# Soft-MoE after attention on one core: last combine weights turned ahead of the stores, two evictions by one engine each, first quarters from two queues, 16 constant products less

## The chip, the cores and the metric

The kernel runs on one core of a Trainium2 chip. The metric is the device time of one execution in microseconds; the median of three runs is given. One further execution was profiled, and all views below are of that one.

## The reference

```python
def attn(q, k, v, cap):                      # (8 batches, 12 heads, 448 rows, 64 columns)
    scores = cap * tanh(q @ k.T / sqrt(64) / cap)
    return softmax(scores) @ v

def soft_moe(x, phi, w1, w2):                # x: 3584 x 768, 8 experts, 4 slots each, F = 1024
    logits = x @ phi                         # 3584 x 32
    d = softmax(logits, axis=0)              # dispatch weights, over the tokens
    slot_in = d.T @ x                        # 32 x 768
    slot_out[e] = relu(slot_in[e] @ w1[e]) @ w2[e]
    c = softmax(logits, axis=1)              # combine weights, over the slots
    return c @ slot_out                      # 3584 x 768, float32
```

The tokens `x` are the attention's output with its heads side by side. The output has 11.0 MB.

## The kernel before

The order of instructions is written out by hand (`tc.manual_schedule()`); the framework adds the semaphore waits. Each engine runs its own list in order: PE (TensorE), DVE (VectorE), ACT (ScalarE), POOL (GpSimd) and SP, which computes nothing and issues DMAs. A DMA issued by SP or ACT signals its landing on one of eight semaphores (DMAHW0 to DMAHW7), which the framework gives out in turn.

**Attention**, to about 245 us. Two heads of a batch make a pair; scores come in 112 chunks of 3 x 448 columns. ACT takes tanh (L325) and exp (L329) of each chunk, DVE takes part of the exp by a polynomial, and PE multiplies scores and values and turns the results. `FILL` lists constant products (`fill`, 57 columns each, L425) that PE does between others: for seven of the batches 38 in one place and 12 in another.

**Per batch b**, `phi` gives logits, ACT their exp `E`, and `e_rep` (POOL, L488) repeats it into the tile `e4`, of which there is one buffer. `e_transp(b)` (L502) turns `e4` by four PE transposes into PSUM (`eps`, L507) and copies it by DVE (L508) into `ET4`, or for the last two batches (`bl - 1` and `bl`, 6 and 7) into `ETl`: these are the combine weights, not yet normalised. `e_sums` (L513) adds them up by seven small products (`wps`, L517) and takes the reciprocal into `winv`. For the last two batches all this is done late: batch 7 first, then `e_rep` builds `e4` of batch 6 anew.

**The slot network**, from about 246 us. `busy(6)` does two constant products of 384 columns while PE waits. `layer1` gives four results `hp` (two groups of four experts by two halves of F); `relu` evicts each into `hbs` (in the tile `small`); the one with `i == half == 1` is split, 288 columns by ACT and 224 by DVE. `h_transp` turns them (`hps`, `hpad`). `layer2(n0, half)` adds up `so_ps[half]`, the slots' output for columns 0 to 383 or 384 to 767, in 16 steps of four products. Their weights are partly kept in SBUF (`w2b`) and partly loaded back from DRAM by 21 DMAs of 384 KB on SP (`w2t`, L824): ten of half 0, then eleven of half 1, the last of them being `n0 = 60` of half 1, which the last step of `layer2` needs.

**The stores.** There are 28 tiles of 128 tokens. For tiles 0 to 11 each half is stored by itself (`half_tile`: one product `op`, one eviction times `winv` by ACT or DVE into `obh`, one DMA of 192 KB on SP from L898). Half 0 of tiles 0 to 9 is done between the steps of `layer2(..., 1)`:

```python
    act.copy(so[0][:, 0:HB], so_ps[0][:, 0:HB])
    dve.tensor_copy(so[0][:, HB:HD], so_ps[0][:, HB:HD])
    ...
        layer2(n0, 1)
        if n0 % 8 == 4 and n0 != n2 // 2 + 4 and done < NHL:
            for eng in ("act", "dve") if n0 < n2 // 2 else ("act",):
                half_tile(done, 0, ...)
```

Half 0 of tile 0 is cut once more into two quarters of 96 KB, one evicted by ACT and one by DVE (L915), both stored by SP (L916). Then come `so[1]` (DVE, L944), half 0 of tiles 10 and 11, and in the last loop half 1 of tiles 0 to 11. Tiles 12 to 27 are done whole: two products, one eviction of 768 columns (ACT L980, DVE L978) into `ob`, and nine DMAs of one or two tiles on SP. In this loop, between tiles, stand `e_transp(7)`, `e_rep(6)`, `e_transp(6)` and `e_sums(3)`.

Of the kernel before, what the change touches and what calls it, by code (L numbers as in the profile page):

```python
# [10 lines left out]
BF16 = mybir.dt.bfloat16  # L11
# [3 lines left out]
ALU = mybir.AluOpType  # L15
ACT = mybir.ActivationFunctionType
PSUM = bass.MemoryType.PSUM

P = 128
HP = 64  # L20
NT = 7
# [16 lines left out]
def kernel(  # L38
# [12 lines left out]
    B, H, _, _ = q.shape  # L51
    D = H * DH
# [4 lines left out]
    HD = D // 2  # L57
# [12 lines left out]
    pe, dve, act, pool, sp = nc.tensor, nc.vector, nc.scalar, nc.gpsimd, nc.sync  # L70

    consts = ctx.enter_context(tc.tile_pool(name="consts", bufs=1))
    wts = ctx.enter_context(tc.tile_pool(name="wts", bufs=1))
    psT = ctx.enter_context(tc.tile_pool(name="psT", bufs=1, space=PSUM))
# [14 lines left out]
    phib = consts.tile([P, NJ, NS], BF16, name="phib")  # L89
    ET4 = consts.tile([P, B // 2 - 1, NT, 2, HP], BF16, name="ET4")  # L90
    winv = consts.tile([P, B // 2, NT], F32, name="winv")
    slT = consts.tile([P, NJ, NS], BF16, name="slT")
    zacc = consts.tile([P, 1], F32, name="zacc")
    rz = consts.tile([P, 1], F32, name="rz")
# [390 lines left out]
    def e_rep(b):  # L485

        e4s[b] = consts.tile([P, NG, 4 * NS], BF16, name="e4", tag="e4", bufs=1)
        pool.tensor_copy(e4s[b].rearrange("p g (a s) -> p g a s", a=4),  # L488
                         es[b].unsqueeze(2).to_broadcast([P, NG, 4, NS]))
# [9 lines left out]
        else:  # L499
            dve.tensor_tensor(zacc, ps, zacc, op=ALU.add)  # L500

    def e_transp(b):  # L502

        ps = psT.tile([P, 512], BF16, name="eps", tag="T")
        for g in range(NG):
            n = P if g < NF else HP
            pe.transpose(ps[:, g * P:g * P + n], e4s[b][0:n, g, :], ident[0:n, 0:n])  # L507
        dve.tensor_copy((ETl if b >= B - 2 else ET4[:, b // 2])[:, :, b % 2, :],  # L508
                        ps[:, 0:S].rearrange("p (c q) -> p c q", q=HP))

    def et_tile(bb, c):
        return (ETl if bb == B // 2 - 1 else ET4[:, bb])[:, c, :, :].rearrange("p a q -> p (a q)")

    def e_sums(bb):
        ps = psT.tile([P, NT], F32, name="wps", tag="T")
        for c in range(NT):
            pe.matmul(ps[:, c:c + 1], et_tile(bb, c), ones32, start=True, stop=True)  # L517
        dve.reciprocal(winv[:, bb, :], ps)
# [34 lines left out]
    def at(j, slot, f, *a):  # L553
        if j < 0:
            j, slot = 0, "b"
        aux.setdefault((j, slot), []).append((f, a))
# [2 lines left out]

        busy(n, psV.tile([P, parts * P], F32, name="junk", tag="pv"))  # L560

    FILL = ((4, 'a', fill, 6), (5, 'a', fill, 6), (6, 'a', spare, 3), (6, 'c', spare, 9), (7, 'a', fill, 38), (8, 'a', fill, 12), (9, 'a', fill, 4),)
    PER = 2 * NQB * NT // CH
    assert PER == 7 and NQB == 3

# [12 lines left out]
    for b in range(B):  # L578
        j, p = b * PER, 6 * b
# [10 lines left out]
        if b == 0:  # L590
            at(j + 1, "d", spare, 34)
            at(j + 2, "d", spare, 4)
        for k, slot, f, n in FILL:
            if (b or k > 2) and j + k < NCH - 1:
# [39 lines left out]
    def busy(n, home=None, by=None):  # L634
        home, by = junk if home is None else home, ones if by is None else by
        if home.shape[-1] > P:
            for _ in range(n // 3):
                pe.matmul(home, ones, wide, start=True, stop=True)
            n, home = n % 3, home[:, 0:P]
        for _ in range(n):  # L640
            pe.matmul(home, by, by, start=True, stop=True)
# [51 lines left out]
    Q, bl = NQ - 1, B - 1  # L693
# [2 lines left out]
    attp.close()  # L696
    mid = ExitStack()
    big = mid.enter_context(tc.tile_pool(name="big", bufs=1, space=PSUM, reuse_waits="tile"))
    turns = [0, 1, 2, 6, 3, 4, 5, 0, 6, 3, 0, 1, 2, 3, 4, 5]

    def bank(shape, dt=F32, name="bank"):
        n = turns.pop(0)
        if not turns:
            turns.extend((3, 2, 6, 0, 1))
        return big.tile(shape, dt, name=name, tag=f"b{n}")
# [84 lines left out]
    phi_last(last - 1, (0, 1, 2))  # L790
    x_last(1, dve.tensor_copy)
    phi_last(last, (0, 1), True)
    busy(6)
    e_last(0)
    phi_last(last, (2,))
    phi_last(last - 1, (NF,))
# [22 lines left out]
    tl = ctx.enter_context(tc.tile_pool(name="tl", bufs=1, reuse_waits="tile"))  # L819
# [6 lines left out]

    hpad = tl.tile([P, E, NFT, NS], BF16, name="hpad")
    pool.memset(hpad, 0.0)
    ETl = tl.tile([P, NT, 2, HP], BF16, name="ETl")

    def w2_half(n, half):
        part = (n - n % 4, half)
        if part in w2t:
# [3 lines left out]
    hbs = {}  # L837
# [8 lines left out]
        return i, half, hp  # L846

    def relu(i, half, hp):
        f0, f1, mid = 512 * half, 512 * half + 512, 512
        if i == half == 1:  # L850
            mid = f0 + 288
        if f0 < mid:
            f2 = min(f1, mid)
            act.activation(hbs[i][:, f0:f2], hp[:, 0:f2 - f0], ACT.Relu, scale=rz)
        if mid < f1:
            f2 = max(f0, mid)
            dve.tensor_scalar(hbs[i][:, f2:f1], hp[:, f2 - f0:512], rz, 0.0, ALU.mult, ALU.max)

    def h_transp(i):

# [10 lines left out]
    so_ps = []  # L871

    def layer2(n0, half):
        for n in range(n0, n0 + 4):
            i, ft, gg = blocks[n]
            pe.matmul(so_ps[half][32 * gg:32 * gg + NS, :],  # L876
                      hpad[:, 4 * i + gg, ft, :],
                      w2_half(n, half),
                      start=(n0 == 0), stop=(n0 == len(blocks) - 4))
# [7 lines left out]
    so = [small[:, 2 * F + n * HD:2 * F + n * HD + HD] for n in range(2)]  # L887
    for hp in first:
        relu(*hp)
# [13 lines left out]
    def half_tile(n, half, home, eng):  # L903

        m = half * NH + n
        if m % 8 == 0:
            obs[m // 8] = own_home([P, 8, HD], F32, "obh")
        ob = obs[m // 8][:, m % 8, :]
        bb, c = divmod(n, NT)
        if n == half == 0:  # L910

            for p, (bank_p, mul) in enumerate(zip(home, (act.mul, dve.tensor_scalar_mul))):
                cs = slice(p * HD // 2, (p + 1) * HD // 2)
                pe.matmul(bank_p, et_tile(bb, c), so[half][:, cs], start=True, stop=True)
                mul(ob[:, cs], bank_p, winv[:, bb, c:c + 1])  # L915
                sp.dma_start(out=bass.AP(tensor=out.tensor, offset=cs.start,  # L916
                                         ap=[[NT * D, P], [1, HD // 2]]), in_=ob[:, cs])
            return
        pe.matmul(home, et_tile(bb, c), so[half], start=True, stop=True)
        if eng == "dve":  # L920
            dve.tensor_scalar_mul(ob, home, winv[:, bb, c:c + 1])
        else:
            act.mul(ob, home, winv[:, bb, c:c + 1])
        store(n, half, half + 1, ob)

    NH, NHL = 12, 10
    n2 = len(blocks)
    for n0 in range(0, n2, 4):
        if n0 == n2 // 2 - 8:
            h_transp(1)  # L930
        layer2(n0, 0)
    HB = HD // 2
    act.copy(so[0][:, 0:HB], so_ps[0][:, 0:HB])
    dve.tensor_copy(so[0][:, HB:HD], so_ps[0][:, HB:HD])
    done = 0
    for n0 in range(0, n2, 4):
        layer2(n0, 1)

        if n0 % 8 == 4 and n0 != n2 // 2 + 4 and done < NHL:
            for eng in ("act", "dve") if n0 < n2 // 2 else ("act",):  # L940
                half_tile(done, 0, bank([P, HD], name="op0") if done else
                          [bank([P, HD // 2], name="op00") for _ in range(2)], eng)
                done += 1
    dve.tensor_copy(so[1], so_ps[1])  # L944
    for done in range(NHL, NH):
        half_tile(done, 0, bank([P, HD], name="op0"), "dve" if done % 2 else "act")
    mid.close()
# [3 lines left out]
    last_ob = None  # L951
    for n in range(B // 2 * NT):
        bb, c = divmod(n, NT)
        if n == NH + 3:
            e_transp(B - 1)
            e_rep(B - 2)
        if n == NH + 5:
            e_transp(B - 2)
        if n == NH + 7:
            e_sums(B // 2 - 1)  # L960
        op = fin.tile([P, 2, 512], F32, name="op", tag="op")
        if n < NH:
            half_tile(n, 1, op[:, 0, 0:HD], "act" if n % 2 else "dve")
            continue
        for half in range(2):
            pe.matmul(op[:, half, 0:HD], et_tile(bb, c), so[half],
                      start=True, stop=True)

        if n == NH or c == 0 or full:
            n1 = n  # L970
            if n in (NH, NH + 4, NH + 8, NH + 11):
                ob, at0 = own_home([P, 4, 2, HD], F32, "ob"), n
                last_ob = ob if n == NH + 8 else last_ob
        if n == B // 2 * NT - 1:
            ob, at0 = last_ob, n - 3
        dst = ob[:, n - at0, :, :]
        if n % 2:
            dve.tensor_scalar_mul(dst, op[:, :, 0:HD], winv[:, bb, c:c + 1])  # L978
        else:
            act.mul(dst, op[:, :, 0:HD], winv[:, bb, c:c + 1])  # L980
        full = n > n1 or c == NT - 1
        if full:
            store(n1, 0, 2, ob[:, n1 - at0:n - at0 + 1, :, :].rearrange("p t a d -> p (t a d)"),
                  n - n1 + 1)
# [35 lines left out]
```

## Time and profile before

| | us |
|---|---|
| median of 3 runs (295.8 to 296.04) | 296.0 |
| the profiled execution, its own time | 295.63 |
| its span, first to last instruction | 293.9 |
| PE busy | 255.3 (87%) |
| DVE busy | 240.0 (82%) |
| ACT busy | 260.1 (89%) |
| POOL busy | 138.6 (47%) |
| mean DMA rate | 232 GB/s |

All times in the views are counted from the span's start. The difference of 1.7 us between span and own time lies around the span. The page cuts the span into 40 slices and gives the busy share of each in tenths. A window's row gives, after its length, the busy time of PE, PEld (weight loads), DVE, ACT and POOL with the number of instructions, the granted PE clock, the DMA share and GB/s. In a source view the three durations are the least, the median and the largest in ns. A name with a q (SPq) is the engine's sequencer, here issuing DMAs.

### The profile page before, as it was taken

The numbers are of one execution on the slowest core, as the hardware profiler recorded it, in microseconds if no ns is written. First come the engines' busy times: TensorE is split into PE (matmuls) and PEld (weight loads), VectorE is DVE, ScalarE is ACT, GpSimd is POOL, SyncE is SP. The second block draws the span as 40 slices with busy tenths as digits, with TensorE's granted clock in tenths as the row PEclk, the third lists the DMA queues.
The fourth block names the chain that finished last, engine by engine and source line by source line (L and its number), as shares of the span: only waits on it lengthen the run. The fifth ranks groups of instructions, "written<-read, shape, count | busy, mean of one in ns | idle before, by whom it ended". The sixth has DMA issues, their size and how long they took to land.

```text
span 293.9 us, 10841 instructions
## 1 busy us (share of the span) xinstructions
PE 255.3 (87%) x4728; PEld 173.8 (59%) x4728; DVE 240.0 (82%) x554; ACT 260.1 (89%) x211; POOL 138.6 (47%) x200
## 2 busy tenths in 40 slices
PE   8898889988998899879988998899989899998800
PEld 6656566756675667556756675667566668542400
DVE  3728998999999999999999989998999976246920
ACT  4999999999999999999999999999999997237710
POOL 4493555763677366735673658375643220300000
PEclk9999999999999999999999999999999999999975
DMA  7999999999999999999999999999999576979996
GB/s 230 249 196 205 221 180 216 199 189 218 229 219 203 204 229 222 203 200 223 193 191 217 209 221 202 217 219 225 209 183 216 108 245 217 406 307 393 356 420 283
DMA packets 58560, 68.13 MB, mean 232 GB/s; under 512 B 4240, under 2 KB 54672, under 8 KB 58512
## 3 DMA queue, kind: packets, MB, share of 16 engines
q0 software_dynamic: 42448, 35.31, 78.1%
q1 hardware_dynamic: 15776, 31.89, 31.1%
q8 instruction: 37, 0.61, 0.8%
q10 hardware_dynamic: 288, 0.23, 0.2%
q14 instruction: 11, 0.09, 0.1%
HBM read 91.72 MB, written 19.27 MB: 378 GB/s over the span
## 4 chain that ended last, share of the span: by engine, by line
DVE 36%; PE 35%; ACT 17%; issue 4%; POOL 2%; DMA 1%; DVEq 0%
PE pv L395 12%; ACT ex L325 8%; ACT ex L329 7%; PE sc L316 6%; DVE xq L405 4%; DVE ex L376 3%; DVE xp L375 3%; DVE xp L372 3%; DVE xp L373 3%; DVE kT L278 3%; DVE ex L369 3%; DVE xp L374 3%; DVE xf L371 2%; DVE qT L278 2%; PE so_ps L876 2%
## 5 line engine op out<-in xcount | busy, mean ns | idle before, releaser
L325 ACT ACTIVATE ex<-sc 128x1344 f16<-128x1344 f32 (+1 forms) x113 | 147.6, 1414 | 1.7 <-PE sc L316 1.6
L329 ACT ACTIVATE ex<-ex 128x1792 bf16<-128x1792 f16 (+5 forms) x58 | 119.7, 2068 | 0.1
L395 PE MATMUL pv<-vbd,ex 128*128 128x130 bf16 (+1 forms) x1610 | 94.5, 211 | 5.7 <-POOL vbd L286 3.2
L395 PEld LDWEIGHTS <-ex 128*128 128x128 bf16 (+1 forms) x1680 | 75.7, 101 | 33.5 <-PE sc L316 7.0
L316 PE MATMUL sc<-qT,kT 64*64 64x448 bf16 x672 | 70.3, 359 | 4.0 <-DVE qT L278 1.6
L286 POOL CAST vbd<-vraw 64x896 bf16<-64x896 f32 x46 | 44.0, 956 | 52.5 <-PE pv L395 37.9
L316 PEld LDWEIGHTS <-kT 64*64 64x64 bf16 x672 | 24.4, 105 | 10.2 <-issue 5.8
L405 DVE TENSOR_TENSOR xq<-pv,rec 128x448 bf16<-128x448 f32 x46 | 28.7, 625 | 1.6
L117 POOL DMA_DIRECT2D w1b<-in_moe_w_dram x32 | 25.3, 792 | 0.0
L488 POOL COPY e<-E 128x512 bf16<-128x512 bf16 x9 | 6.4, 708 | 37.1 <-PE eps L507 19.7
L376 DVE TENSOR_TENSOR ex<-ex,xp 128x896 uint16<-128x896 uint16 (+1 forms) x39 | 21.8, 559 | 1.2
L294 POOL MEMSET vbd<- 64x1 bf16 x22 | 3.1, 139 | 41.1 <-PE pv L395 41.1
L375 DVE TENSOR_TENSOR xp<-xp,xf 128x896 f16<-128x896 f16 (+1 forms) x39 | 22.0, 563 | 0.4
L373 DVE TENSOR_TENSOR xp<-xp,xf 128x896 f16<-128x896 f16 (+1 forms) x39 | 21.6, 554 | 0.7
L276 PE MATMUL qps<-ident,qb 128*64 128x128 bf16 x308 | 12.8, 221 | 8.8 <-DVE kT L278 6.4
L278 DVE COPY kT<-kps 128x896 bf16<-128x896 bf16 x23 | 14.3, 622 | 6.2 <-PE kps L276 5.8
L372 DVE TENSOR_SCALAR xp<-xf 128x896 f16<-128x896 uint16 (+1 forms) x39 | 18.9, 484 | 0.5
L276 PEld LDWEIGHTS <-qb 128*64 128x64 bf16 x308 | 10.9, 109 | 14.0 <-issue 13.5
L425 PE MATMUL pv<-ones 128*128 128x57 bf16 x474 | 18.6, 188 | 0.0
L186 POOL DMA_DIRECT2D qb<-in_q_dram x22 | 16.7, 761 | 3.2 <-DMA kraw<-in_k_dram 3.2
L457 DVE COPY xT<-xps 128x896 bf16<-128x896 bf16 (+1 forms) x24 | 14.4, 598 | 3.3 <-PE xps L448 3.1
L121 POOL DMA_DIRECT2D w2d<-in_moe_w_dram x21 | 16.4, 811 | 0.0
(135 smaller groups left out, 365.1 us busy)
## 6 DMA issues: line engine op xcount, KB each, us to landing
w1b<-in_moe_w_dram POOLq DMA_DIRECT2D x32, 384.0 KB, 8.4
vraw<-in_v_dram SPq DMA_DIRECT2D x44, 224.0 KB, 6.0
w2d<-in_moe_w_dram POOLq DMA_DIRECT2D x21, 384.0 KB, 8.9
w2t<-w2d SPq DMA_DIRECT2D x21, 384.0 KB, 7.2
out_dram<-ob SPq DMA_DIRECT2D x7, 768.0 KB, 7.8
qb<-in_q_dram POOLq DMA_DIRECT2D x22, 224.0 KB, 7.3
kb<-in_k_dram POOLq DMA_DIRECT2D x22, 224.0 KB, 6.1
out_dram<-obh SPq DMA_DIRECT2D x23, 192.0 KB, 2.1
```

Of the source, the lines that this page charges most:

```text
L117: pool.dma_start(out=w1b[e][:, js, fs], in_=w1r[:, e, js, fs])
L278: dve.tensor_copy(t, ps)
L286: pool.tensor_copy(vbds[Q % 2][r, :, :, c0:c0 + DH], raw[r])
L316: pe.matmul(sc[cs, u, 0:S], qkT["k", Q][r, c, cs], qkT["q", Q][r, :, cs], start=True, stop=True)
L325: act.activation(exs[j][:, half * CS + u0:half * CS + u1, :].bitcast(F16), sc[:, u0:u1, 0:S], ACT.Tanh, scale=qk_scale / cap)
L329: act.activation(exs[j][:, u0:u1, :], exs[j][:, u0:u1, :].bitcast(F16), ACT.Exp, scale=cap)
L372: lambda: dve.tensor_scalar(p, f, c3, c2, ALU.mult, ALU.add),
L373: lambda: dve.tensor_tensor(p, p, f, op=ALU.mult),
L375: lambda: dve.tensor_tensor(p, p, f, op=ALU.mult),
L376: lambda: dve.tensor_tensor(y, y, p, op=ALU.add),
L395: pe.matmul(out_, exs[j][r, u, q0:q0 + (HP if tail else P)], v_, start=(c == 0 and g == gs[0] < NF), stop=(c == NT - 1), skip_group_check= ...
L405: dve.tensor_tensor(xq[Q][:, h, s0:s1, :], pv[:, 0:s1 - s0, 0:DH], rec.to_broadcast([P, s1 - s0, DH]), op=ALU.mult)
```

## The change

- The two last combine weights are turned earlier: `e_transp(6)` takes the place of `busy(6)`, before `e4` is overwritten; `e_transp(7)` stands between the copy of `so[0]` and the first store, and `e_sums(3)` behind the copy of `so[1]`, ahead of tiles 10 and 11. The second `e_rep(6)` goes. `ETl` moves to another pool.
- The relu of `i == half == 1` and the copy of `so[0]` are each ACT's alone.
- The first quarter's store is issued by ACT, the second's by SP.
- Half 0 of tiles 0 to 9 stands ahead of two steps of `layer2(..., 1)` instead of behind them.
- `FILL` has 37 and 11 products for 38 and 12, in seven batches each. With the two of `busy(6)` that makes 16 products less in the program (or 20, counted in units of 128 columns for those two).

```diff
+    ETl = consts.tile([P, NT, 2, HP], BF16, name="ETl")
...
-    def e_transp(b):
-        ps = psT.tile([P, 512], BF16, name="eps", tag="T")
+    def e_transp(b, ps=None):
+        if ps is None:
+            ps = psT.tile([P, 512], BF16, name="eps", tag="T")
...
-    FILL = (... (7, 'a', fill, 38), (8, 'a', fill, 12), (9, 'a', fill, 4),)
+    FILL = (... (7, 'a', fill, 37), (8, 'a', fill, 11), (9, 'a', fill, 4),)
...
-    turns = [0, 1, 2, 6, 3, 4, 5, 0, 6, 3, 0, 1, 2, 3, 4, 5]
+    turns = [0, 1, 2, 6, 3, 4, 5, 0, 6, 3, 2, 0, 1, 2, 3, 4, 5]
...
-    busy(6)
+    e_transp(bl - 1, bank([P, 512], BF16, name="eps"))
...
-    ETl = tl.tile([P, NT, 2, HP], BF16, name="ETl")
...
     def relu(i, half, hp):
-        f0, f1, mid = 512 * half, 512 * half + 512, 512
-        if i == half == 1:
-            mid = f0 + 288
-        ...
+        dst = hbs[i][:, 512 * half:512 * half + 512]
+        if i or not half:
+            act.activation(dst, hp, ACT.Relu, scale=rz)
+        else:
+            dve.tensor_scalar(dst, hp, rz, 0.0, ALU.mult, ALU.max)
...
-                sp.dma_start(out=bass.AP(tensor=out.tensor, offset=cs.start,
+                (act, sp)[p].dma_start(out=bass.AP(tensor=out.tensor, offset=cs.start,
...
-    HB = HD // 2
-    act.copy(so[0][:, 0:HB], so_ps[0][:, 0:HB])
-    dve.tensor_copy(so[0][:, HB:HD], so_ps[0][:, HB:HD])
+    act.copy(so[0], so_ps[0])
+    e_transp(bl)
     for n0 in range(0, n2, 4):
-        layer2(n0, 1)
-        if n0 % 8 == 4 and n0 != n2 // 2 + 4 and done < NHL:
+        if n0 % 8 == 0 and n0 != n2 // 2 and done < NHL:
             for eng in ("act", "dve") if n0 < n2 // 2 else ("act",):
                 half_tile(done, 0, ...)
+        layer2(n0, 1)
     dve.tensor_copy(so[1], so_ps[1])
+    e_sums(bl // 2)
...
-        if n == NH + 3:
-            e_transp(B - 1)
-            e_rep(B - 2)
-        if n == NH + 5:
-            e_transp(B - 2)
-        if n == NH + 7:
-            e_sums(B // 2 - 1)
```

More of the change, by code (lines that the diff above doesn't have):

```diff
@@ L560, in spare @@
         busy(n, psV.tile([P, parts * P], F32, name="junk", tag="pv"))
-    FILL = ((4, 'a', fill, 6), (5, 'a', fill, 6), (6, 'a', spare, 3), (6, 'c', spare, 9), (7, 'a', fill, 38), (8, 'a', fill, 12), (9, 'a', fill, 4),)
+    FILL = ((4, 'a', fill, 6), (5, 'a', fill, 6), (6, 'a', spare, 3), (6, 'c', spare, 9), (7, 'a', fill, 37), (8, 'a', fill, 11), (9, 'a', fill, 4),)
     PER = 2 * NQB * NT // CH
@@ L848, in relu @@
     def relu(i, half, hp):
-        f0, f1, mid = 512 * half, 512 * half + 512, 512
-        if i == half == 1:
-            mid = f0 + 288
[L852 to L857, printed above, removed]
+        dst = hbs[i][:, 512 * half:512 * half + 512]
[3 more added lines that the diff above has]
+            dve.tensor_scalar(dst, hp, rz, 0.0, ALU.mult, ALU.max)
     def h_transp(i):
@@ L915, in half_tile @@
                 mul(ob[:, cs], bank_p, winv[:, bb, c:c + 1])
-                sp.dma_start(out=bass.AP(tensor=out.tensor, offset=cs.start,
-                                         ap=[[NT * D, P], [1, HD // 2]]), in_=ob[:, cs])
+                (act, sp)[p].dma_start(out=bass.AP(tensor=out.tensor, offset=cs.start,
+                                                   ap=[[NT * D, P], [1, HD // 2]]), in_=ob[:, cs])
             return
```

## The prediction

> **What bounds the kernel now.** I read the page first (slices, queues), then windows of one microsecond over the last stage, then the timeline and the source views of the stores.
>
> ```profile
> ACT  4999999999999999999999999999999997237710
> DMA  7999999999999999999999999999999576979996
> q8 instruction: 37, 0.61, 0.8%
> ```
>
> The last line gives packets, MB and share of queue 8. Up to about 245 us ScalarE is full (its exp and tanh groups, L325 and L329, show 1.7 and 0.1 us of idle time), so nothing done to TensorE there can gain much. The last stage is the one that changes, and it ends 13 us after the last arithmetic (DVE L978 ends at 280.9): it is the draining of stores that sets the end.
>
> ```profile
> 260.00:261.00 1.00, 0.90 (x21) 0.40 (x10) 0.24 (x1) 0.32 (x1) 0.00 (x0) 1.00 1.02 412
> 262.00:263.00 1.00, 1.00 (x16) 0.29 (x12) 0.91 (x2) 0.58 (x1) 0.00 (x0) 1.00 0.38 123
> 263.00:264.00 1.00, 1.00 (x12) 0.23 (x10) 0.72 (x2) 0.58 (x1) 0.00 (x0) 1.00 0.31 103
> 267.00:268.00 1.00, 0.83 (x3) 0.23 (x4) 1.00 (x3) 0.68 (x2) 0.00 (x0) 1.00 1.07 398
> 274.00:275.00 1.00, 0.75 (x12) 0.39 (x11) 1.00 (x3) 0.43 (x1) 0.00 (x0) 1.00 0.14 40
> 276.50:291.00 14.50, 2.68 (x14) 1.10 (x12) 3.98 (x5) 3.48 (x4) 0.00 (x0) 0.70 1.02 421
> ```
>
> The last two numbers are DMA share and GB/s. There are two holes: 261.5 to 264, between the last w2 load and the stores, and 274 to 275. From 276.5 to 291 the 16 DMA engines are full, so the end moves by what the first whole-tile store (`ob`, now issued at 275.56) moves. What sets that:
>
> ```profile
> L916 SPq DMA_DIRECT2D out_dram<-obh x2: 338/708/1079, 261.5 to 261.9; - x2
> DMA to landing us min/median/max: 2.2/2.3/2.4
> L898 SPq DMA_DIRECT2D out_dram<-obh x20: 381/408/418, 263.1 to 272.6; - x20
> L898 SPq DMA_DIRECT2D out_dram<-obh x5: 383/416/1404, 272.1 to 275.0; - x5
> q8 instruction: 1, 0.02, 5.5%
> q8 instruction: 1, 0.02, 5.9%
> ```
>
> SP issues one 192 KB store each 0.50 us (0.41 for the issue, 0.09 for the wait before it), which is 393 GB/s, just what the windows show; the evictions are 0.3 to 3.5 us ahead. So SP's issue queue is the bound from 263.1 to 275.5. Two of its issues are long: 1.08 us at 261.94 and 1.40 at 273.06. In just these two windows (261.6 to 262.7, 272.7 to 274.1; the last two lines) one packet of kind "instruction" was under way, none between. Both issues end 0.4 us after that packet. I read 37 packets of 16 KB against 9,486 TensorE instructions (4,728 products, as many weight loads, 30 waits, drains and branches) as one packet for each 256. The second long issue costs 1.40 - 0.41 = 0.99 us and is the hole at 274.
>
> **The change, part by part.** The sum is made in the profiled execution: span 293.9, its own time 295.63; the median of the runs is 296.0, so differences are added to 296.0.
>
> *Constant products.* The two lists of instructions differ by 16 products: 14 of 57 columns in attention (starts 27 ns apart, 0.38 us of TensorE in all) and 2 of 384 columns at 249.5. Attention is ScalarE's, so the 14 are worth 0, at most 0.4 by ScalarE's idle time; a loss would need a lower clock, and the granted clock is 1.00 in every window until 282. The 2 are replaced by 4 transposes (0.47 us busy at L507, the two 0.48), both under the wait for DVE's `xT` copy (249.57 to 249.83); their DVE copy (0.38) falls at 250.0 to 250.4, where DVE is idle until 251.1. Sum 0; uncovered, each would cost up to its duration.
>
> *One relu by ACT.* Before, ACT takes 288 columns (257.24, 0.50), then DVE 224 (0.45, ends 258.22). ACT alone takes 0.69 for 512 columns (L854 at 255.54) and would end at 257.93. TensorE is busy with `so_ps` products until 257.99 and now starts the transposes at 258.09: gain 0.10.
>
> *One copy by ACT.*
>
> ```profile
> 260.41 0.32 ACT L933 CAST small<-so_ps 128x192 bf16<-128x192 f32 x1 [2.67 <-PE so_ps L876]
> 260.76 0.36 DVE L934 CAST small<-so_ps 128x192 bf16<-128x192 f32 x1 [1.94 <-ACT small L933]
> 261.06 0.42 ACT L915 ACTIVATE obh<-op,winv 128x192 f32<-128x192 f32 x1 [0.33 <-PE op L914]
> 261.45 0.42 DVE L915 TENSOR_SCALAR obh<-op,winv 128x192 f32<-128x192 f32 x1 [0.33 <-PE op L914]
> ```
>
> The two halves ran one after the other. 384 columns on ACT: 0.32 plus the 0.16 by which L923 (0.58, 384 columns) exceeds L915 (0.42, 192) = 0.48. The whole ends at 260.41 - 0.10 + 0.48 = 260.79 instead of 261.12. The first quarter is evicted by 261.54 (now 261.48), the second by 261.62 (261.87), and the next tiles some 0.25 to 0.45 earlier, since they also move ahead of 8 `so_ps` products. The transposes of `e_transp(bl)` fill TensorE meanwhile, and the copy of ETl (260.5 to 260.9) is done before DVE's first eviction.
>
> *Weights at the end.* 8 transposes, 7 small products, two DVE copies (0.38 each), one reciprocal (0.20) and one POOL copy (0.61) leave the stretch 272 to 275.5. Evictions are ahead of SP there: worth 0. Put ahead of tile 10, the 7 products and the reciprocal delay it by 0.3, ready about 267.6 for an issue now at 267.55; this decides only if SP runs early, and it does not:
>
> *The first quarter on ACT's queue.* It frees SP of one issue (0.34 to 0.44). The Trainium skill (DMA: Bandwidth & Descriptors, section "Issuing engines are not separate DMA queues") says that a second issuing engine saves only the sequencer's issue time; by that rule this part would be a gain of 0.4; no run here shows it yet. But it adds a wait. SP's and ACT's DMAs take eight completion semaphores in turn, and each waits until the former user of its own has landed. In the new list ACT's quarter has DMAHW2, and so has the last w2 load on SP (`w2t` for n0=60, second half), which waits for 144 = the 128 reached before and the quarter's 16. That load stands on SP ahead of every other store. Now it is issued at 255.35; then it waits until the quarter has landed in DRAM, with the second quarter and all `obh` and `ob` stores queued behind it.
>
> Issue on ACT at 261.58; landing after 2.2 us (L916; L898's least is 1.9, the largest 2.4) gives 263.8. If ACT's issue falls into an instruction packet, as SP's did at 261.94, it comes up to 0.7 later. Then on SP the load's issue (0.34) and the second quarter's (0.38), with 0.09 before each: tile 1 at 264.7, where it is 263.1 now: **+1.6** (1.2 to 2.1). The long issue at 261.94 is not paid again, it falls into the wait. The load's 384 KB (0.93 us at 415 GB/s) now fall into the hole, at least half of them before stores come: **+0.2** (0 to 0.45). `w2t` lands 3.1 us after its issue at the least (tile view of `w2t`; 7.2 in the median, in a full queue), by 266.9; TensorE wants it at 266.1, tile 10 becomes ready at 268.2, SP issues it at 269.2: covered by 1 us.
>
> *The last instruction packet.* It came 60 TensorE instructions before number 9,472 = 37 x 256. The new list has 9,454 (16 products and 16 weight loads less), so a 37th block would not be needed. If it goes, the 0.99 us goes: **-1.0**.
>
> Sum: +1.6 + 0.2 - 1.0 = **+0.8, 296.8 us**. What is late next is still SP: `ob` at 276.2 rather than 275.56.
>
> **Rivals.**
> 1. *The packet stays* (some tens of instructions that the list leaves out, or a fetch past the end). Two "instruction" packets of q14 after 280 us, when little code is left, speak for it; the count 37 x 256 against it. A stall of 0.8 to 1.3 then hits SP as now, and swallows the load's backlog: +1.6, **297.6**.
> 2. *The packet never was the cause.* The overlap is shown in two stores only. The Trainium skill (Runtime: NRT & Kernel Launch, section "Instruction fetch mechanics") states that crossing a 16 KiB block costs one tail-bump, mostly hidden, which the 1.40 beside 0.41 us does not bear out; by it fewer instructions gain nothing. Some stall of that size would stay: 297.6 as in rival 1, and I count them together.
> 3. *Faster: SP is not held.* If the semaphore is reached before SP needs it, tile 1 goes at 262.2, tile 10 at 267.6 binds, and with the packet gone `ob` comes at 274.6: -1.0, **295.0**. The point: the quarter would have to land by 261.2, before it can be issued, so only a reading of the list that is wrong allows it. If only the packet stays besides: **296.0**, no change.
> 4. *The late load becomes the bound.* At the 7.5 us that `w2t` takes in a full queue it lands at 271.4; the second halves then start near 272.8 instead of 267.4, `ob` near 279: **299.5**. Only three DMAs are in flight then, which speaks against it.
>
> **How the numbers follow.** Forecast 0.52; rivals 1 and 2 together 0.29; rival 3 faster 0.08, without change 0.05; rival 4 0.04; the rest 0.02. A measurement here tells 0.2%, 0.6 us, from no change. The forecast alone runs from +0.2 to +1.4 (landing and backlog); about a quarter of it lies within 0.6. Faster 0.09, same 0.18, slower 0.73. The range 295.6 to 297.9 holds the forecast, the unchanged case and nearly all of rivals 1 and 2, and leaves out rival 4 and the faster case.
>
> **What would show it.** Right: a long wait of SP ahead of the last `w2t` load, ended by ACT's quarter landing near 263.8; DMA idle to 264.5; tile 1 near 264.7; 36 packets on q8, no issue over 1 us from 265 to 276, no hole at 274; `ob` from 276.2. Wrong: the last `w2t` load issued before 261, or tile 1 before 263; a 37th packet makes rival 1.

## The result, and the profile after

| | before | after |
|---|---|---|
| median | 296.02 us (20 runs) | 297.86 us (20 runs) |
| ratio | | 1.0069, 95% interval [1.0042, 1.0096] |
| last `exp` of attention starts | 246.67 | 248.84 |
| tile 1 issued by SP | 263.11 | 266.74 |
| first `ob` issued by SP | 275.56 | 279.65 |
| span | 293.9 | 298.4 |

The change costs 1.8 us by the medians and 2.0 by the ratio. The profiled execution of after (its own time 300.14, 2.3 above the median) is 2.26 us behind before's already at 24 us, which the change does not explain (e1, with the same edits up to there, is 0.0 behind); so its times are compared after taking off 2.17, the difference at the last `exp`. What is left is 1.46 at tile 1, 0.46 between tile 1 and the first `ob` and 0.41 behind it.

The page of after, DMA by slices and the queue of the instruction packets (packets, MB, share):

```profile
DMA  7989999999999999999999999999999558949996
q8 instruction: 37, 0.61, 0.8%
```

There are still 37 packets, and the 4 among the slices (261 to 269 us) is where before had a 7 (257 to 265). The last stage in windows (PE, PEld, DVE, ACT, POOL, PE clock, then DMA share and GB/s):

```profile
263.00:264.00 1.00, 0.82 (x11) 0.49 (x12) 0.62 (x2) 0.67 (x2) 0.00 (x0) 1.00 0.17 59
264.00:265.00 1.00, 1.00 (x18) 0.23 (x10) 0.91 (x3) 0.47 (x2) 0.00 (x0) 1.00 0.00 1
266.00:267.00 1.00, 1.00 (x22) 0.45 (x18) 0.75 (x2) 0.67 (x2) 0.00 (x0) 1.00 0.31 52
271.00:272.00 1.00, 0.71 (x3) 0.30 (x4) 1.00 (x3) 0.58 (x2) 0.00 (x0) 1.00 1.07 399
278.00:279.00 1.00, 0.89 (x6) 0.38 (x4) 1.00 (x2) 0.77 (x1) 0.00 (x0) 1.00 0.76 270
```

The hole has grown: the DMA engines move nothing at 264 and little until 267, where in before (its times plus 2.17) they had a third of their rate from 264 to 266 and were full from then on. The second hole, at 278, is still there, but shallower: 270 GB/s where before had 40 at 274. Why the first grew, in the waits of SP between 255 and 282 us (us in total, times, longest):

```profile
SPq L826 <- DMA out_dram<-obh: 7.9, 1, 7.9
```

A load from DRAM (L826, the last `w2t`) waited 7.9 us for a store to land: the quarter that ACT issued. The issues themselves (start, length, line), ACT's list first, then SP's:

```profile
262.88 0.48 ACT L928 CAST small<-so_ps 128x384 bf16<-128x384 f32 x1 [2.44 <-PE so_ps L872]
263.69 0.42 ACT L911 ACTIVATE obh<-op,winv 128x192 f32<-128x192 f32 x1 [0.33 <-PE op L910]
264.14 0.35 ACTq L912 DMA_DIRECT2D out_dram<-obh  x1
```

```profile
255.68 10.49 SPq L826 DMA_DIRECT2D w2t<-w2d  x4
266.27 0.38 SPq L912 DMA_DIRECT2D out_dram<-obh  x1
266.74 12.81 SPq L894 DMA_DIRECT2D out_dram<-obh  x23
279.65 3.30 SPq L894 DMA_DIRECT2D out_dram<-ob  x4
```

The four loads of the first row end at 266.17, so the last one was issued at 265.85, 1.71 us behind ACT's issue. Then the 23 stores of half tiles, 12.81 us for them (12.35 in before). Two views of their issues, 264 to 272 and 276 to 279 us, and the queue of packets from 276.9 to 278.3 us:

```profile
L894 SPq DMA_DIRECT2D out_dram<-obh x10: 382/432/677, 266.7 to 271.9; - x10
DMA to landing us min/median/max: 2.7/3.2/3.4
L894 SPq DMA_DIRECT2D out_dram<-obh x5: 382/407/1196, 275.9 to 278.7; - x5
q8 instruction: 1, 0.02, 4.9%
```

In the first, two issues of 0.67 and 0.68 us (at 268.80 and 271.11) are new. In the second, the 37th packet makes an issue of 1.20 us, as it did in before (1.40).

### The profile page after: what moved, and what is told of

The parts are those of the page before. It is cut to its first block, busy times and chain, and to the rows that moved or that the text cites. A ratio compares the mean times of both kernels' runs of the same rounds, so it can differ in the third digit from the quotient of the medians.

```text
span 298.4 us, 10805 instructions
## 1 busy us (share of the span) xinstructions
PE 258.4 (87%) x4712; PEld 174.7 (59%) x4712; DVE 240.0 (80%) x552; ACT 260.9 (87%) x211; POOL 137.5 (46%) x199
## 4 chain that ended last, share of the span: by engine, by line
PE 37%; DVE 31%; ACT 18%; DMA 4%; issue 4%; POOL 2%; DVEq 0%; POOLq 0%; SPq 0%
PE pv L396 11%; ACT ex L326 9%; ACT ex L330 7%; PE sc L317 7%; DVE xq L406 4%; DVE ex L377 3%; DVE kT L279 3%; DVE xp L374 3%; DVE xp L376 2%; DMA vraw<-in_v_dram 2%; DVE xp L373 2%; DVE ex L370 2%; DVE xp L375 2%; DVE xf L372 2%; DVE qT L279 2%
## 5 line engine op out<-in xcount | busy, mean ns | idle before, releaser
L317 PE MATMUL sc<-qT,kT 64*64 64x448 bf16 x672 | 72.1, 365 | 3.0 <-DVE qT L279 1.6
L373 DVE TENSOR_SCALAR xp<-xf 128x896 f16<-128x896 uint16 (+1 forms) x39 | 18.1, 465 | 0.5
L426 PE MATMUL pv<-ones 128*128 128x57 bf16 x460 | 18.3, 188 | 0.0
L372 DVE TENSOR_SCALAR xf<-ex 128x896 uint16<-128x896 uint16 (+1 forms) x39 | 17.0, 437 | 0.3
L187 POOL DMA_DIRECT2D kb<-in_k_dram x22 | 16.2, 735 | 0.6 <-PE kps L277 0.5
```

The costliest lines, as they stand in the source:

```text
L187: pool.dma_start(out=t, in_=quad_ap(nm, Q))
L317: pe.matmul(sc[cs, u, 0:S], qkT["k", Q][r, c, cs], qkT["q", Q][r, :, cs], start=True, stop=True)
```

## The experiments

Theory: SP is held by a semaphore that ACT's quarter and the last `w2t` load share (the lane wait, in the expectations); the late load of 384 KB then lies as a backlog ahead of the stores; and an instruction packet under way holds an issue of SP. Rivals: the loss is in the other parts of the change; a second queue costs by itself; the packet has no part in it. All results in one table: median, ratio to before with its interval; then from the profile the packets on q8, the time from the last `exp` to tile 1, from there to the first `ob`, and from there to the end of the span.

| run | us | ratio | packets | to tile 1 | to `ob` | to the end |
|---|---|---|---|---|---|---|
| before | 296.0 | 1 | 37 | 16.44 | 12.45 | 18.3 |
| after | 297.86 | 1.0069 [1.0042, 1.0096] | 37 | 17.90 | 12.91 | 18.7 |
| e1, quarter on SP | 295.86 | 0.9997 [0.9966, 1.0027] | 37 | 15.89 | 13.21 | 18.3 |
| e2, before with ACT's quarter | 297.50 | 1.0050 [1.0021, 1.0080] | 37 | 17.44 | 13.02 | 18.3 |
| e3, quarter on GpSimd | 296.62 | 1.0025 [1.0002, 1.0048] | 37 | 15.74 | 13.26 | 18.7 |
| e4, fewer layer2 | 296.48 | 1.0033 [1.0007, 1.0060] | 36 | 17.60 | 12.06 | 18.6 |
| e5, last load on GpSimd | 297.39 | 1.0071 [1.0045, 1.0097] | 37 | 17.17 | 13.09 | 18.8 |
| e8, 35 products less | 297.43 | 1.0056 [1.0031, 1.0082] | 36 | 18.29 | 12.10 | 18.4 |
| e6, no last packet | 294.94 | 0.9977 [0.9956, 0.9999] | 36 | 16.76 | 11.49 | 18.4 |
| e7, moved only | 296.79 | 1.0025 [1.0000, 1.0050] | 37 | 16.77 | 12.07 | 18.3 |
| e9, pairs | 296.00 | 0.9987 [0.9962, 1.0013] | 37 | 16.29 | 10.76 | 20.7 |
| e10, pairs, no packet | 294.77 | 0.9942 [0.9914, 0.9971] | 36 | 16.76 | 9.57 | 19.9 |

**e1: only the queue undone.**

```diff
-                (act, sp)[p].dma_start(out=bass.AP(tensor=out.tensor, offset=cs.start,
+                sp.dma_start(out=bass.AP(tensor=out.tensor, offset=cs.start,
```

> The changed kernel with both quarters issued by SP again; all else of the change stays. Theory (the lane wait): the last w2t load no longer shares a semaphore with the first quarter, so SP issues it near 255.5 and goes on at 261.5 with the quarters; tile 1 at 262.3 to 262.7 (the changed kernel: 266.7 in a profile that was 2.2 us late before the stage), 37 instruction packets on q8, first ob at 275.4 to 275.8, time 295.7 to 296.3, that is 1.000 of before (0.998 to 1.002). Rival (the loss is in the other parts: the two evictions by one engine, the weights turned ahead, the tiles ahead of layer2): nearly all of the loss stays, 297.3 to 298.1, ratio 1.005 to 1.007.

The whole loss is gone, and the parts left change the time, taken together, by nothing that can be told. SP's timeline, 254 to 282 us:

```profile
254.12 1.24 SPq L826 DMA_DIRECT2D w2t<-w2d  x2
261.65 0.81 SPq L912 DMA_DIRECT2D out_dram<-obh  x2
262.56 13.11 SPq L894 DMA_DIRECT2D out_dram<-obh  x23
```

The loads are through at 255.36 and tile 1 is even 0.55 us earlier than in before, since here the 36th packet (260.84 to 261.80) is nearly over when the first quarter is issued (261.65). SP gives that back: 0.6 us of waiting for tile 10 (issued at 267.62 where its slot was 267.02) and a longer issue at the 37th packet (1.65 us).

**e2: only the queue, in the kernel before.** The same edit the other way round.

> The kernel before with one edit: the first quarter's store is issued by ACT. Its last w2t load then takes the same semaphore as that quarter, too. Theory: SP is held ahead of the last w2t load until the quarter has landed, tile 1 comes 1.2 to 1.8 us later than in before (263.1), time 297.2 to 298.0, ratio 1.004 to 1.007. Rival (loss elsewhere): the edit frees SP of one issue, 295.6 to 296.1, ratio 0.998 to 1.000.

```profile
SPq L824 <- DMA out_dram<-obh: 7.8, 1, 7.8
264.21 12.92 SPq L898 DMA_DIRECT2D out_dram<-obh  x23
```

As the theory has it, the 7.8 us wait appears with this one edit, tile 1 comes at 264.21 (263.11; 1.1 later, a little under the 1.2 expected), one early issue takes 0.83 us, and the time rises by 0.5%. With e1 (0.0%) that makes 0.5 of the 0.7%, and the intervals cover the rest.

**e3: a second queue without a shared semaphore.**

```diff
-                (act, sp)[p].dma_start(
+                (pool, sp)[p].dma_start(
```

> The changed kernel with the first quarter issued by GpSimd in place of ACT: still a second queue, but its completion is counted on a semaphore of the software queue, which no load of SP shares. Theory (the shared semaphore, not the second queue, costs): last w2t load near 255.5, tile 1 at 261.9 to 262.4, time 295.5 to 296.2, ratio 0.998 to 1.001. Rival (a store of 96 KB on another queue hurts by itself, by its descriptors or by its place among the DMAs): 297 or more, ratio 1.004 or more.

The trace does what the theory says: no wait, tile 1 at 262.21, 0.35 us ahead of e1's, about one issue of SP. The Trainium skill (DMA: Bandwidth & Descriptors, section "Issuing engines are not separate DMA queues") gives a second engine just this, the issue time, and this trace agrees. The time does not: 296.6, between the two expectations, 0.8 above e1 by the medians, with intervals that overlap. In the profiled execution (295.93, below the median) SP loses the 0.35 again by waiting for tile 10 (issued at 267.57, in e1 at 267.62), and the end comes 1.55 us behind the last landing, where it is 1.15 to 1.19 in the other runs with single stores and without a DMA of GpSimd in the last stage; 0.34 of it is one pause between two of SP's last waits. What makes that pause, and the rest of the 0.8, stay open.

**e4: TensorE's list made shorter behind the first stores.**

```diff
-        layer2(n0, 1)
+        if n0 % 16 == 0 or n0 == n2 - 4:
+            layer2(n0, 1)
```

> The changed kernel, in which 11 of the 16 steps of layer2 for the second half are left out (44 products and 44 weight loads, all but one behind the first stores; the second half of the output is not complete). TensorE's list falls to 9366 instructions, below the place (record 9409) at which the 37th packet began. Theory (the packet holds SP's issue): 36 instruction packets, no store issue over 0.8 us between 270 and the first ob, ob 0.7 to 1.1 us earlier than in the changed kernel, time 296.7 to 297.3, ratio 1.0025 to 1.0045. Rival (the packet goes and nothing else, or the long issue has another cause): a long issue of about 1.2 us stays in that stretch, 297.6 to 298.1, ratio 1.006 to 1.007.

The page's packets, and SP's issues from 263 to 275.9 us:

```profile
q8 instruction: 36, 0.59, 0.8%
L894 SPq DMA_DIRECT2D out_dram<-obh x23: 383/407/685, 263.9 to 275.5; - x23
```

The packet is gone and so is the long issue; the time falls by 1.4 us against after (1.1 by the ratios), which puts the ratio within the theory's range and the median 0.2 below it. What remains beyond 0.45 are two issues of 0.69 and 0.66 us, the backlog of the late load: its 23 stores take 0.6 us longer than those of e6, which has neither.

**e5: the shared semaphore moved on by one DMA.**

```diff
-        sp.dma_start(out=t, in_=w2d[n0, half])
+        (pool if (n0, half) == (60, 1) else sp).dma_start(out=t, in_=w2d[n0, half])
```

> The changed kernel, with the last w2t load issued by GpSimd in place of SP; ACT still issues the first quarter. The next SP DMA that shares the quarter's semaphore is now the second quarter's store, so SP is still held, but no load of 384 KB comes late. Theory (lane wait plus backlog of the late load): SP goes on when the first quarter has landed, 263.0 to 263.4, tile 1 at 263.5 to 263.9, every store issue before the 37th packet takes 0.38 to 0.45 us (the long ones of 0.66 to 0.83 us in the changed kernel and in the two kernels with a late load are gone), ob 0.8 to 1.0 us earlier than in the changed kernel, time 296.6 to 297.1, ratio to before 1.003 to 1.0045. Rival (the long issues come from something else, such as two queues with stores at once): they stay, 297.3 to 297.7, ratio 1.005 to 1.0065.

```profile
SPq L912 <- DMA out_dram<-obh: 8.0, 1, 8.0
L894 SPq DMA_DIRECT2D out_dram<-obh x23: 382/407/2038, 263.7 to 276.3; - x23
```

Now the second quarter waits for the first, as foretold (until 263.25), and no issue is long but one, so the two long ones do come from the late load. The time is a miss all the same: 297.4. The 37th packet took 1.55 us here and the issue beside it 2.04, which gives back 0.8 of what was won. By the ratios nothing is won against after (1.0071 to 1.0069). The end comes 1.58 us behind the last landing, with the pause seen in e3.

**e8: 35 constant products less in attention.** `FILL` has 34 and 9 in place of 37 and 11.

> The changed kernel with 35 more constant products of attention left out (34 and 9 in FILL), 70 TensorE instructions before the last stage. The list is then 9384 long, and the 37th packet, which began at record 9401 to 9413 in four profiles, should not come. Theory (a packet holds SP wherever it falls): 36 packets; no long issue at the end of the half-tile stores, but the 36th now begins some 70 instructions later, at 264 to 266 beside SP's first stores, and holds one of those for 0.5 to 1.2 us; the sum is 0 to -0.8 against the changed kernel, 297.0 to 298.0, ratio 1.004 to 1.007. Rival (only the number of packets counts): -1.0 or more, 296.4 to 296.9, ratio 1.002 to 1.003. Rival (the packet has nothing to do with it): a long issue stays near 274 to 277, 297.7 to 298.0.

```profile
L912 ACTq DMA_DIRECT2D out_dram<-obh x1: 353/353/353, 261.9 to 261.9; - x1
DMA to landing us min/median/max: 2.3/2.8/3.3
L894 SPq DMA_DIRECT2D out_dram<-obh x23: 383/408/777, 265.2 to 276.8; - x23
```

The 37th packet and its long issue are gone (12.10 against 12.91 us to `ob`), but the 36th now begins at 262.26, under way while ACT's quarter is: it lands after 2.3 us where it took 1.7 in after, e2, e4 and e5. SP waits for it, so the packet is paid there, and attention ended 0.3 us later. 0.4 us of gain are left. The place differed from the one expected, the sum did not.

**e6 and e7: no packet beside the stores.** From e1, work that needs neither loaded weights nor `so[0]` is put ahead of the first store; e6 also has fewer products, so that the 36th packet stays in place and the 37th is not needed.

```diff
+        if n0 == n2 - 8:
+            e_transp(bl)
         layer2(n0, 0)
+        if n0 == n2 - 8:
+            for k in (0, 4):
+                layer2(k, 1)
     act.copy(so[0], so_ps[0])
-    e_transp(bl)
+    for k in (8, 12, 16):
+        layer2(k, 1)
+    e_sums(bl // 2)
...
-        layer2(n0, 1)
+        if n0 > 16:
+            layer2(n0, 1)
...
-    FILL = (... (7, 'a', fill, 37), (8, 'a', fill, 11), ...)
+    FILL = (... (7, 'a', fill, 34), (8, 'a', fill, 10), ...)     # e6 alone
```

> Both quarters issued by SP; five steps of layer2 for the second half that need no loaded weights (40 instructions) and the seven sums of the last combine weights (14) stand ahead of the first store in place of behind it, and 28 more constant products are left out (34 and 10 in FILL), so that the 36th packet stays where it was and the list ends at 9398. Theory: 36 packets, the last one over by 262.0; first quarter at 261.9 to 262.3 (0.3 to 0.6 later than with the quarters on SP alone), no wait of SP for tile 10 (0.6 there) and no long issue (1.24 there): ob at 274.3 to 274.9, time 294.3 to 295.1, ratio 0.994 to 0.997. Rival (the packet comes all the same, or the bytes set the end): 295.5 to 296.2, ratio 0.998 to 1.001.

> As the run without the last packet, but with the constant products of the changed kernel (37 and 11), so the list has 9454 instructions. Theory (the packet holds SP): 37 packets, a long issue of 1.2 to 1.7 us in SP's run between 268 and 275, ob at 275.3 to 276.2, time 295.3 to 296.2, 0.8 to 1.3 us more than the run without the last packet. Rival (the gain of that run comes from the moved steps): within 0.3 us of that run.

First e6 (its packets, its 23 stores and its issues), then e7's:

```profile
q8 instruction: 36, 0.59, 0.8%
263.14 11.38 SPq L894 DMA_DIRECT2D out_dram<-obh  x23
L894 SPq DMA_DIRECT2D out_dram<-obh x23: 381/410/413, 263.1 to 274.1; - x23
```

```profile
L894 SPq DMA_DIRECT2D out_dram<-obh x23: 381/408/1030, 265.9 to 277.5; - x23
```

In e6 all 23 issues take between 0.38 and 0.41 us: nothing stands in SP's way any more, and it is 0.7 us faster than before by the ratio (0.9977, just outside the 0.994 to 0.997 expected; the median, 294.94, was within its range). e7 differs by 28 small products alone, is 1.9 us slower by the medians (1.4 by the ratios), which is more than the 0.8 to 1.3 expected, and has the packet and an issue of 1.03 us. That profile explains 0.6 of it. The rest is not shown: the hold may be longer in other executions (the long issues of the profiles take 1.03 to 2.04), and e7's runs scatter from 295.2 to 298.07, where ten of e6's twelve lie between 294.56 and 295.04.

**e9 and e10: half tiles stored in pairs**, e9 from e1, e10 from e6.

```diff
-        store(n, half, half + 1, ob)
+        if m < 2:
+            store(n, half, half + 1, ob)
+        elif m % 2:
+            o = [(2 * b1 * S + c1) * D + half * HD for b1, c1 in (divmod(n - 1, NT), divmod(n, NT))]
+            sp.dma_start(out=bass.AP(tensor=out.tensor, offset=o[0],
+                                     ap=[[NT * D, P], [o[1] - o[0], 2], [1, HD]]),
+                         in_=obs[m // 8][:, m % 8 - 1:m % 8 + 1, :])
```

> Both quarters issued by SP, and the 22 half tiles from the third on are stored in pairs, 384 KB for each DMA (11 issues in place of 22), each issued when the second of the two is evicted. Theory (SP's issue queue, one DMA each 0.50 us, is the bound of the half-tile stores): the DMA engines now set the pace, 415 to 425 GB/s in place of 393 (0.7 us less over 4.3 MB), and since SP is ahead, the stall by the 37th packet (1.2 us with the quarters on SP alone) is at least half covered by work already queued: time 294.0 to 295.2, ratio 0.993 to 0.997. Rival (the DMA engines or the evictions are the bound already): 295.6 to 296.4, ratio 0.999 to 1.002.

> The run without the last packet (five steps of layer2 and the seven sums ahead of the first store, 28 constant products less) with the 22 half tiles stored in pairs besides. Theory (two separate costs of SP's queue: its pace and the packet): 293.8 to 294.6, ratio 0.990 to 0.994; the packet's removal is worth less here than its 0.8 to 1.9 us with single stores, since pairs cover part of the stall. Rival (the bytes set the end by now): 294.7 to 295.2, ratio 0.996 to 0.998, as with single stores.

Windows of e10, of e9 and, with single stores, of before:

```profile
267.00:275.00 8.00, 6.34 (x29) 2.61 (x29) 6.85 (x11) 6.54 (x11) 0.00 (x0) 1.00 1.07 399
270.00:274.00 4.00, 3.29 (x16) 1.38 (x15) 2.91 (x6) 3.62 (x6) 0.00 (x0) 1.00 1.07 400
264.00:272.00 8.00, 7.00 (x56) 2.55 (x55) 5.19 (x10) 6.08 (x11) 0.00 (x0) 1.00 1.05 392
```

In e9 the rival was right. With half the issues SP runs ahead, and the rate rises from 392 to 399 (e10) and 400 GB/s (e9) only: for these stores the DMA engines are full, too, at about 400. So SP's issue queue, which the prediction had as the bound of this stretch, holds the stores back by 2% at most where no issue is long. Pairs win nothing in e9 (e1's time; the DMA engines stand at 0.69 to 0.85 of full from 267 to 270 us, where stores wait for tile 10 and the next), and in e10 0.2 us on e6 by the medians and 1.0 by the ratios, whose intervals overlap: that is not settled. e9 has a 37th packet, too (275.00 to 275.97), but by then whole tiles are queued, and no issue stands out beside it (0.85 and 1.05 us, with 0.70 and 1.02 in e10). e10 is the fastest kernel of the study, 0.6% faster than before.

## Why the prediction was right or wrong

The direction and the main mechanism were right; the sum of +0.8 was 1.0 to 1.2 too small, and the time is at the upper end of its range, where rivals 1 and 2 stood. (By its sum the first `ob` was due at 276.4, where the text has 276.2; in after it is issued at 277.48, less the 2.17.) The sizes below are read in profiles, one for each kernel.

| term | predicted | found, and where |
|---|---|---|
| attention, relu, copy, weights turned ahead | 0 | 0.0 in sum (e1: ratio 0.9997) |
| wait of SP for the quarter, at tile 1 | +1.6 | +1.46 (after's profile), +1.16 (e4's) |
| backlog of the late load | +0.2 | +0.53 (two issues of 0.67 and 0.68 for 0.41 each); 0.6 to 0.8 up to the last landing (e8, e4 against e6) |
| last instruction packet | -1.0 | -0.2 (issue of 1.20 for 1.40; the packet stays) |

**The step that failed** is "The last instruction packet": "The new list has 9,454 ..., so a 37th block would not be needed." The packet stayed; rival 1 was what happened. The packet holds SP as the text said: e4, e6, e8 and e10 lack the packet and the long issue together. What was wrong is the length of list from which a 37th packet comes. Counting TensorE's recorded instructions up to the start of the 37th packet gives 9,399 to 9,413 in the eight profiles that have it: 59 to 73 short of 9,472. The list of 9,454 passes that point; 9,398 (e6, e10), 9,384 (e8) and 9,366 (e4) do not, so the limit lies between 9,398 and 9,454. The prediction itself read that in before the packet "came 60 TensorE instructions before number 9,472" and did not draw the conclusion that a list ending 18 short of it would trigger it as well. Why the limit lies there stays open: other packets start behind their number (in before the 34th to the 36th by 42, 68 and 30), so the counts do not tell a fetch that runs ahead from some tens of instructions that the list leaves out, the two readings in rival 1.

**The packet as the cause** was rival 2's question. At the 37th packet of before, after, e1, e2, e3, e5 and e7 the long issue ends 0.35 to 0.40 us behind the packet's end, and lasts 1.03 to 2.04 us; without the packet it is gone. The Trainium skill (Runtime: NRT & Kernel Launch, section "Instruction fetch mechanics") has block crossings cost one tail-bump, mostly hidden. What a crossing costs TensorE no run here was made to show; for SP the traces speak against it, and the measurement decides: rival 2 is out.

**The backlog** was mis-sized because the text had the load move at 415 GB/s. More than half of its packets are through before the first store's packet (75 of 128 in after), as the text had it. But they start at 266.82 only, behind the issue of tile 1, and with nothing else under way they come at half that rate while the DMA engines show as full (single packets take up to 0.91 us, the median 0.12), from 266.8 to 267.8 us:

```profile
266.80:267.80 1.00, 1.00 (x21) 0.29 (x13) 0.36 (x1) 0.39 (x2) 0.00 (x0) 1.00 1.10 206
```

The stores do not make that up: they reach 399 GB/s (e10) to SP's 392, and the queue stays filled. The landing times show it: a half tile's store lands after 3.2 us in the median in after (266.7 to 271.9), after 2.0 in e1 (262.6 to 267.6 us):

```profile
DMA to landing us min/median/max: 1.8/2.0/2.1
```

The load is still being paid for at the first `ob`, which lands after 4.55 us in after and 4.03 in before; 0.39 of the 0.41 us behind its issue lie ahead of the last landing. From tile 1 to the last landing e4 takes 29.47 us and e8 29.32, both with the late load and without the 37th packet, e6 28.70 without either: 0.6 to 0.8 for the load. After, with both, takes 30.44, so the packet adds 1.0 to 1.1, much as its long issue in before.

**The lane wait** had two errors that nearly cancel, in part by luck. The landing takes 1.7 us, not 2.2: the 2.2 to 2.4 of before had the 36th packet beside it (e8 shows the same: 2.3). And ACT's issue came 0.4 later than worked out: 264.14 less 2.17 is 261.97, not 261.58. Of that, 0.3 belongs to this one profile, whose first relu is already that much late (7.88 us behind the last `exp`, 7.54 in before, 7.58 in e4); e4, with the same list up to the first quarter, has the term at 1.16. A packet under way at ACT's issue (263.39 to 264.35) did not lengthen it (0.35), which the text had feared; in after the 36th packet costs nothing.

**Parts costed at nothing.** They come to nothing in sum, but not one by one, which is luck in part: in e1 tile 1 is 0.55 earlier because the 36th packet no longer meets the second quarter's issue, and tile 10 is 0.6 late. The whole copy took 0.48 us, as worked out; the 0.10 from the relu does not show (the copy starts at 260.40 in e1, 260.41 in before). `e_sums` ahead of tile 10 delays it until 267.6, as the text had it; covered in after, but in e1 SP waits 0.6 us for it: rival 3's second case ("If only the packet stays besides: 296.0") gives the time of e1, 295.86. Rival 4 did not come: the late load made TensorE wait 0.6 us, and SP issued tile 10 at 271.88, a microsecond after it was ready (270.85).

**Left open:** why the 37th packet comes with a list of 9,454; 1.3 of the 1.9 us between e6 and e7; the pause of 0.34 us in SP's last waits in e3 and e5, both with a DMA of GpSimd added to the last stage, and the rest of what these two are slower than expected.

## What to carry to other kernels

Before giving a DMA to another engine's queue, look up which DMA uses its completion semaphore next, and on which engine: that one waits for the landing (7.9 us in after), with everything queued behind it, even if the two have nothing to do with each other. Where stores set the end, look for issues that are longer than their neighbours and for what is under way on the DMA engines in that moment; here an instruction packet was moved out of the way, or saved, by a few dozen instructions. A saving in one place is only kept if what is shifted with it (here the packet before) does not land in another bad place.

## What the runs showed of the hardware

- The 36th instruction packet of 16 KB, ahead of the half-tile stores, takes 0.88 to 0.96 us (1.17 in e6), the 37th, beside the stores, 0.97 to 1.55. With half tiles queued, a store that SP issues in that time is held until 0.35 to 0.40 us after the packet's end (seven profiles); beside the whole tiles of e9 no hold shows. At the first stores the first issue passes and the second is held: in e3 the packet lasts from 261.33 to 262.29, the issue at 261.69 takes 0.34 us and the one at 262.21 0.44.
- A store of 96 KB that was issued 0.2 to 0.3 us before such a packet began landed 0.6 us later (2.2 in before, 2.3 in e8, for 1.7); the one that e3 issued 0.36 us after the packet's start landed after 1.68.
- The 37th packet comes with lists of 9,454 recorded TensorE instructions and more, and not with 9,398 and fewer; in the eight profiles that have it, it starts 59 to 73 recorded instructions before number 9,472.
- A load of 384 KB that finds nothing else under way moves at 206 GB/s (after, 266.8 to 267.8 us); the same loads one behind the other move at 413 (before, 252 to 260 us).
- Half tiles (rows of 1,536 bytes) are written at 399 GB/s with a full queue (e10), the later whole tiles at 424 (after, 280 to 293 us):

```profile
280.00:293.00 13.00, 2.38 (x11) 0.86 (x9) 3.67 (x4) 2.76 (x4) 0.00 (x0) 0.75 1.03 424
```
